# Pairing the value products of windowed attention and moving two batches' masks from TensorE to VectorE

## The chip, the cores and the metric

The kernel is one program on one core of a Trainium2 chip. The metric is device time in microseconds (us), the median of repeated runs of the whole program; a separate profiled execution gives the trace. Five engines work side by side: TensorE (PE in the profile, with its weight loads as PEld), VectorE (DVE), ScalarE (ACT), GpSimd (POOL) and SyncE (SP), which issues the DMAs.

## The reference

Three layers follow one another, all in float32, on 4 batches of 576 tokens.

1. Attention with 8 heads of 64 dimensions. A query sees only keys at or before its own position: in heads 0 to 3 the last 32 positions, in heads 4 to 7 every fourth of the last 128. `scores = where(mask, q k^T / 8, -1e9)`, softmax over the keys, times `v`.
2. A gated channel layer: `x_prev` is `x` shifted by one token; `xk = mu_k x + (1 - mu_k) x_prev`, `xr` alike with `mu_r`; `k = relu(xk w_k)`, `v = k^2 w_v`, result `sigmoid(xr w_r) * v`.
3. A mixer: `u = x + (relu(x^T w_tok1) w_tok2)^T`, result `u + relu(u w_ch1) w_ch2`.

## The kernel before

**Attention in units.** The dilated heads are stored with their tokens sorted by position modulo 4, so that every head has a plain window of 32 keys. Queries are cut into blocks of 64 (`QB`); a block needs 96 keys (`KB`). A unit is four blocks of pairs of heads; `UNITS` lists nine units for each of the four batches, 36 in all, in the order of `RUNS`. `attend(i, ...)` records one unit:

- two DMAs bring queries and keys (`unit`, 416 KB, ring `unit_r`) and values (`vs`, 192 KB, ring `v_r`);
- one bfloat16 matmul of an identity with a slice of `masks` writes 0 or -1e30 into the unit's score bank `sp` (384 columns, line 558), and four float32 matmuls of 96 columns add the scores on top (line 561);
- VectorE takes the negated row maximum (line 565), ScalarE the exponentials with the row sums into `sm` (lines 578 to 582); every second unit of the first batch does this in three wide operations instead; then come the reciprocal and the product `sm * 1/sum` on VectorE;
- four TensorE transposes write `tp`, `copy` brings it to SBUF as `pt`, a ring of two slots (line 592);
- eight matmuls (`vs` by `pt`, 96 rows by 64 columns, lines 595 to 601) write the values' product into `xp`, 256 columns of one bank. Each float32 matmul appears as two records in the trace, so these eight are 16 records. `nc.burst(start)` keeps them in one piece and adds 0.33 to the planner's cost of the first;
- copies bring `xp` to `xT[b, p]`, in the order of tokens (lines 603 to 615).

**The second layer** walks over six chunks of 384 tokens (`CHUNKS`). `prep(c, which, kt)` makes the two shifted mixes of a chunk from `xT` and splits each into a high and a low float32r part; `keys(c, m)`, `mix(c, m, j)` and `receptance(c, j)` multiply with three float32r products for each float32 one (`mm3`). The units of batch 0 come ahead of it; those of the other three are laid beside it by the table `beside` (lines 728 to 731): batch 1 over steps 0 to 9, batch 2 over 10 to 20, batch 3 over 21 to 33, eight steps to a chunk. Chunk 1 needs the first seven units of batch 1, chunk 4 the first seven of batch 3. After step 10 the score bank, the transpose bank and the value bank are one PSUM bank each (lines 725, 741).

**The third layer** follows (lines 769 to 942); its weights are split into high and low parts as their slots come free.

**The order.** Nothing is issued where it is written. Each call is noted as an operation with its dependencies (`Plan.either`), and `Plan.order` simulates the five engines with a table of costs: every TensorE operation has a due time from the written order, every other one the latest time that still serves the operations that need it, and each engine takes the ready operation with the earliest due time. `nc.early` shifts due times (line 549 for the units' DMAs). A burst's first operation takes over the dependencies of the whole group. All instructions are issued from line 392, so groups in the profile are told apart by tile names and shapes: `bank<-x,at 96*64` are the value products from batch 1 on (`x<-wr` and `x<-z` in batch 0), `bank<-cst,at` the transposes, `bank<-at 128x384 bf16` the masks, `bank<-at 128x96` the scores; `bank<-z,wk`, `bank<-wv,z` and `bank<-wr,z` are the second layer.

Of the kernel before, what the change touches and what calls it, by code (L numbers as in the profile page):

```python
# [15 lines left out]
ALU = mybir.AluOpType  # L16
# [6 lines left out]
QB = 64  # L23
# [3 lines left out]
NBLK = 4  # L27
UQ = NBLK * 2 * QB
UK = NBLK * QB + 2 * W
UV = NBLK * 2 * D  # L30
# [11 lines left out]
RUNS = [  # L42
    [(2, 0, 4)], [(2, 4, 4)], [(2, 8, 1), (3, 0, 3)], [(3, 3, 4)], [(3, 7, 2), (0, 0, 2)],
    [(1, 0, 4)], [(0, 2, 4)], [(1, 4, 4)], [(0, 6, 3), (1, 8, 1)],
]
# [7 lines left out]
FIRST = [sum(TILES[:c]) for c in range(len(CHUNKS))]  # L53
CH = 512
NEG = -1.0e30

SLOTS = dict(
    cst=[160], xt=[584] * 12, x2=[2048] * 2 + [1024] * 5, at=[3536, 784, 1216],
# [347 lines left out]
def tile_model(nc, banks, units, cst, mu, w_k, w_v, w_r, w_t1, w_t2, w_c1, w_c2, outT):  # L406
# [14 lines left out]
    def cut(name, numbers, size, count=None):  # L421

        out = []
        for n in numbers:
            out += [(name, n, size * i) for i in range(SLOTS[name][n] // size)]
        return out[:count]

    def ring(*places):
        return Ring(at, sum((p if isinstance(p, list) else [p] for p in places), []))

    def psum(*numbers):
        return Ring(bank, numbers)
# [7 lines left out]
    def copy(out, in_):  # L440
        nc.either(
            ("scalar", "activation", dict(out=out, in_=in_, func=AF.Copy)),
            ("vector", "tensor_copy", dict(out=out, in_=in_)),
        )

    def combine(out, in0, in1, op):
        nc.vector.tensor_tensor(out=out, in0=in0, in1=in1, op=op)
# [86 lines left out]
    masks = table[:, :len(TABLE) * KB // 2].halves().split(len(TABLE), KB)  # L534
    ident_h = table[:, len(TABLE) * KB // 2:].halves()
    unit_r = ring(cut("wv", range(4), UQ + UK), ("z", 4, 0))
    v_r = ring(cut("wr", range(4), UV), ("z", 4, UQ + UK))
# [4 lines left out]
    def attend(i, s_ring, t_ring, x_ring):  # L542

        b, runs = UNITS[i]
        unit, vs = unit_r.tile(UQ + UK), v_r.tile(NBLK, 2, D)[:KB]
        values = units[i][:KB, UQ + UK:].rearrange("p (a b c) -> p a b c", a=NBLK, b=2)
        for out, in_ in ((unit, units[i][:, :UQ + UK]), (vs, values)):
            nc.sync.dma_start(out=out, in_=in_)
            nc.early[len(nc.ops) - 1] = {0: 30, 1: -45}.get(b, 0)
        blocks, o = [], UQ  # L550
        for p, j0, n in runs:
            if j0 == 0:
                nc.gpsimd.memset(out=xT[b, p][:, 0:1], constant=0.0)
            blocks += [(p, j0 + j, unit[:, o + QB * j:o + QB * j + KB]) for j in range(n)]
            o += QB * n + W
        sp, sm, st = s_ring.tile(NBLK, KB), sm_r.tile(NBLK, KB), st_r.tile(4, NBLK)
        row = ROWS[i % len(RUNS)]
        nc.tensor.matmul(out=sp, lhsT=ident_h, rhs=masks[:, row:row + NBLK, :], start=True, stop=False)
        for n, (p, j, ks) in enumerate(blocks):
            qs = unit[:, 2 * QB * n:2 * QB * n + 2 * QB]  # L560
            nc.tensor.matmul(out=sp[:, n, :], lhsT=qs, rhs=ks, start=False, stop=n == NBLK - 1)
            if b:
                nc.early[len(nc.ops) - 1] = -0.5 * n
        scale = 1.0 / np.sqrt(D)
        nc.vector.tensor_reduce(
            out=st[:, 0, :], in_=sp, axis=mybir.AxisListType.X, op=ALU.max, negate=True
        )
        if b == 0 and i % 2:
            nc.vector.tensor_tensor(out=sm, in0=sp, in1=st[:, 0, :].wide(KB), op=ALU.add)
            nc.scalar.activation(out=sm, in_=sm, func=AF.Exp, scale=scale)  # L570
            nc.vector.tensor_reduce(out=st[:, 2, :], in_=sm, axis=mybir.AxisListType.X, op=ALU.add)
        else:
            nc.either(
                ("vector", "tensor_scalar", dict(
                    out=st[:, 1, :], in0=st[:, 0, :], scalar1=scale, scalar2=None, op0=ALU.mult)),
                ("scalar", "activation", dict(out=st[:, 1, :], in_=st[:, 0, :], func=AF.Copy, scale=scale)),
            )
            for j in range(NBLK):
                nc.scalar.activation(
                    out=sm[:, j, :], in_=sp[:, j, :], func=AF.Exp, scale=scale,  # L580
                    bias=st[:, 1, j:j + 1], accum_out=st[:, 2, j:j + 1],
                )
        nc.either(
            ("vector", "tensor_scalar_add", dict(out=st[:, 2, :], in0=st[:, 2, :], scalar1=1e-9)),
            ("scalar", "activation", dict(out=st[:, 2, :], in_=st[:, 2, :], func=AF.Copy, bias=1e-9)),
        )
        nc.vector.reciprocal(out=st[:, 3, :], in_=st[:, 2, :])
        combine(sm, sm, st[:, 3, :].wide(KB), ALU.mult)
        tp, pt = t_ring.tile(NBLK, 2 * QB)[:KB], pt_r.tile(NBLK, 2 * QB)[:KB]
        for j in range(NBLK):  # L590
            nc.tensor.transpose(out=tp[:, j, :], in_=sm[:, j, :], identity=ident)
        copy(pt, tp)
        xp = x_ring.tile(QB * NBLK)
        start = len(nc.ops)
        for j in range(NBLK):
            for hh in range(2):
                r = slice(64 * hh, 64 * hh + 64)
                nc.tensor.matmul(
                    out=xp[r, QB * j:QB * j + QB], lhsT=vs[:, j, hh, :], rhs=pt[:, j, r],
                    start=True, stop=True,  # L600
                )
        nc.burst(start)
        o = 0
        for p, j0, n in runs:
            x, t, end = xT[b, p][:, 1:], QB * j0, QB * (j0 + n)
            if p < 2:
                copy(x[:, t:end], xp[:, o:o + end - t])
                o += end - t
                continue
            x = x.split(S // 4, 4).swap()  # L610
            while t < end:
                c, k = divmod(t, S // 4)
                m = min(end - t, S // 4 - k)
                copy(x[:, c, k:k + m], xp[:, o:o + m])
                t, o = t + m, o + m
# [71 lines left out]
    def mix(c, m, j):  # L687
# [16 lines left out]
        out=om_sb, in0=mu_sb, scalar1=-1.0, scalar2=1.0, op0=ALU.mult, op1=ALU.add  # L704
    )
    diag = []
    for which in range(2):
        diag.append([])
        for kt in range(4):
            diag[which].append([])  # L710
            for k, factor in enumerate((om_sb, mu_sb)):
# [3 lines left out]
                        out=d, in0=ident, scalar1=factor[:, col], scalar2=None, op0=ALU.mult)),  # L715
# [3 lines left out]
    s_ring, t_ring, x_ring = psum(0, 3, 5), psum(1, 6), psum(2, 7)  # L719
    n_units = len(UNITS) // B  # L720
    for i in range(n_units):
        attend(i, s_ring, t_ring, x_ring)


    s_ring, t_ring, x_ring = psum(0, 4), psum(1), psum(2)
    unit_r = ring([("at", 0, (UQ + UK) * i) for i in range(2)])
    v_r = ring([("at", 0, 2 * (UQ + UK) + UV * i) for i in range(3)])
    beside = {}
    for n, (lo, hi) in enumerate(([0, 20], [20, 42], [42, 68])):
        for i in range(n_units):  # L730
# [4 lines left out]
    for g in range(8 * nchunk + 2):  # L735
# [22 lines left out]
        for h in beside.get(2 * g, []):  # L758
            attend(h, s_ring, t_ring, x_ring)
# [5 lines left out]
        for h in beside.get(2 * g + 1, []):  # L765
            attend(h, s_ring, t_ring, x_ring)
# [117 lines left out]
    uhl, mid, op = {}, {}, {}  # L884
# [89 lines left out]
def _constants():  # L974
# [4 lines left out]
    def cut(n):  # L979

        return band & ((i < n) | (j >= W + n))

    first = cut(0)
    blocks = [first, band, cut(16), cut(32), cut(48), cut(-16)]
    masks = np.hstack([np.where(blocks[n], 0.0, NEG) for n in TABLE])
    ident = np.eye(128, dtype=np.float32)
# [34 lines left out]
```

## Time and profile before

| | us |
|---|---|
| median of 3 runs | 734.55 (733.45 to 735.19) |
| the profiled execution | 732.79 |
| its span, first to last instruction | 731.0 |
| PE busy | 715.6 |
| DVE busy | 404.7 |
| ACT busy | 287.1 |

Busy times are unions of an engine's instructions. Matmuls overlap in the profile (one of 384 columns is drawn 0.34 us long while the next starts much earlier), so a matmul's cost is read from the distance between starts, not from its length. The profiled execution lies 1.76 us under the median; 1.79 us of it lie outside the span.

### The profile page before, as it was taken

Reading aid. Unit: us, or ns where it says so; the run is one execution under the profiler, and the core shown is the slowest. Engines: PE = TensorE matmul, PEld = TensorE weight load, DVE = VectorE, ACT = ScalarE, POOL = GpSimd, SP = SyncE. Lnnn points to the kernel's source line nnn. Section 1 sums busy time; section 2 is a strip of 40 time slices with the busy share of each in tenths; the row PEclk is TensorE's granted clock in tenths of the full one; section 3 lists DMA queues with packets and bytes.
Section 4 is the critical chain, followed back from the end, with each engine's and each line's share of the span. In section 5 each row is a group of like instructions: output and inputs, shape, how many; then the busy total and the mean of one; then the engine's idle time right before and its main releaser. Section 6 shows DMA issues by size and latency. Waiting matters only on the chain.

```text
span 731.0 us, 10615 instructions
## 1 busy us (share of the span) xinstructions
PE 715.6 (98%) x4124; PEld 604.6 (83%) x4124; DVE 404.7 (55%) x917; ACT 287.1 (39%) x803; POOL 1.2 (0%) x20
## 2 busy tenths in 40 slices
PE   7699999999999999999999999999999999999998
PEld 6578888888888888988878888888888888888897
DVE  6898898387477388786788898132114112211121
ACT  5776775356244354464466543120112011011110
POOL 0000000000000000000000000000000000000000
PEclk9799999999999999999999999999999999999999
DMA  8946632214122100203321342001000000100010
GB/s 293 323 156 225 196 132 81 67 52 144 47 68 70 46 16 22 73 30 105 98 81 54 96 127 76 1 0 58 1 0 23 35 1 1 57 1 0 1 59 30
DMA packets 26082, 53.84 MB, mean 74 GB/s; under 512 B 2480, under 2 KB 10032, under 8 KB 26032
## 3 DMA queue, kind: packets, MB, share of 16 engines
q1 hardware_dynamic: 26032, 53.17, 22.9%
q8 instruction: 32, 0.52, 0.3%
q14 instruction: 18, 0.15, 0.1%
HBM read 48.44 MB, written 4.72 MB: 73 GB/s over the span
## 4 chain that ended last, share of the span: by engine, by line
PE 95%; DMA 4%; SPq 0%; issue 0%; DVE 0%
PE bank L392 95%; DMA at<-units 2%; DMA wr<-units 1%; DMA wv<-units 1%; SPq L392 0%; DVE z L392 0%
## 5 line engine op out<-in xcount | busy, mean ns | idle before, releaser
L392 PE MATMUL bank<-z,wk 128*128 128x384 f32 (+2 forms) x816 | 196.4, 358 | 0.0
L392 DVE SCALAR_TENSOR_TENSOR z<-bank,z 128x512 fp32r<-128x512 f32 (+2 forms) x116 | 70.4, 607 | 222.3 <-ACT z L392 221.5
L392 ACT ACTIVATE z<-bank 128x512 fp32r<-128x512 f32 (+3 forms) x123 | 65.0, 529 | 285.3 <-PE bank L392 284.3
L392 PEld LDWEIGHTS bank<-z,wk 128*128 128x128 f32 x816 | 146.9, 188 | 15.1 <-ACT x L392 0.3
L392 PE MATMUL bank<-wv,z 128*128 128x512 f32 x432 | 128.9, 405 | 0.0
L392 PE MATMUL bank<-z,x 128*128 128x512 f32 (+1 forms) x540 | 120.2, 371 | 0.0
L392 PEld LDWEIGHTS bank<-z,x 128*128 128x128 f32 x540 | 94.9, 188 | 18.7
L392 PEld LDWEIGHTS bank<-wv,z 128*128 128x128 f32 x432 | 78.3, 189 | 13.8
L392 PE MATMUL bank<-z,at 128*128 128x512 f32 (+2 forms) x300 | 76.9, 388 | 0.0
L392 PE MATMUL bank<-wr,z 128*128 128x512 f32 x216 | 62.8, 406 | 0.0
L392 PEld LDWEIGHTS bank<-z,at 128*128 128x128 f32 (+1 forms) x300 | 52.6, 188 | 11.3 <-issue 1.3
L392 PE MATMUL bank<-at 128*128 128x96 f32 (+1 forms) x252 | 46.3, 284 | 11.0 <-DMA at<-cst 4.9
L392 ACT ACTIVATE at<-bank,at 128x96 f32<-128x96 f32 x128 | 42.4, 340 | 23.7 <-PE bank L392 11.6
L392 DVE TENSOR_TENSOR z<-z,z 128x384 fp32r<-128x384 f32 x88 | 48.1, 554 | 5.8 <-ACT z L392 2.6
L392 PE MATMUL bank<-xt,wk 128*128 128x512 f32 (+2 forms) x176 | 45.2, 387 | 0.0
L392 PEld LDWEIGHTS bank<-wr,z 128*128 128x128 f32 x216 | 39.2, 189 | 6.6
L392 PEld LDWEIGHTS bank<-at 128*128 128x128 f32 x216 | 35.3, 195 | 8.0 <-DMA at<-units 4.1
L392 PE MATMUL bank<-at,z 128*128 128x288 f32 x192 | 35.9, 306 | 0.0
L392 PEld LDWEIGHTS bank<-xt,wk 128*128 128x128 f32 x176 | 30.5, 192 | 6.1
L392 ACT ACTIVATE z<-z 128x384 fp32r<-128x384 f32 x57 | 29.5, 522 | 14.3 <-DVE z L392 8.3
L392 ACT ACTIVATE x<-bank 96x512 f32<-96x512 f32 (+1 forms) x41 | 24.2, 594 | 27.1 <-PE bank L392 26.9
L392 PEld LDWEIGHTS bank<-at,z 128*128 128x128 f32 x192 | 29.7, 188 | 4.0 <-issue 1.8
(106 smaller groups left out, 787.2 us busy)
## 6 DMA issues: line engine op xcount, KB each, us to landing
at<-units SPq DMA_DIRECT2D x27, 416.0 KB, 3.7
wr<-w_c SPq DMA_DIRECT2D x20, 512.0 KB, 3.6
at<-units SPq DMA_DIRECT2D x27, 192.0 KB, 2.6
x<-w_k SPq DMA_DIRECT2D x4, 1024.0 KB, 6.9
x<-w_v SPq DMA_DIRECT2D x4, 1024.0 KB, 7.0
wv<-units SPq DMA_DIRECT2D x8, 416.0 KB, 6.6
outT<-z SPq DMA_DIRECT2D x9, 256.0 KB, 2.0
x<-w_r SPq DMA_DIRECT2D x4, 512.0 KB, 3.6
```

What stands on the lines that cost most here:

```text
L392: call(kw["out"], kw["constant"]) if method == "memset" else call(**kw)
```

## The change

From batch 1 on, `attend` no longer multiplies its own values: it puts the unit on a list, and `weigh` writes the products of two units into the two halves of one bank in one burst (`TOGETHER = 2`; a batch's ninth unit goes alone). In batches 2 and 3 (`MASKED = 2`) the mask matmul is left out; VectorE adds the mask to the scores and writes them to `sm` in SBUF, and the maximum and the exponentials then read `sm`. The ring of the values gets a fourth slot, `y`.

```diff
+MASKED = 2
+TOGETHER = 2
...
-        nc.tensor.matmul(out=sp, lhsT=ident_h, rhs=masks[:, row:row + NBLK, :], start=True, stop=False)
+        mask = masks[:, row:row + NBLK, :]
+        by_pe = b < MASKED
+        if by_pe:
+            nc.tensor.matmul(out=sp, lhsT=ident_h, rhs=mask, start=True, stop=False)
         for n, (p, j, ks) in enumerate(blocks):
             qs = unit[:, 2 * QB * n:2 * QB * n + 2 * QB]
-            nc.tensor.matmul(out=sp[:, n, :], lhsT=qs, rhs=ks, start=False, stop=n == NBLK - 1)
+            nc.tensor.matmul(out=sp[:, n, :], lhsT=qs, rhs=ks, start=not by_pe, stop=n == NBLK - 1 or not by_pe)
...
         scale = 1.0 / np.sqrt(D)
+        if not by_pe:
+            nc.vector.tensor_tensor(out=sm, in0=sp, in1=mask, op=ALU.add)
+            sp = sm
         nc.vector.tensor_reduce(
             out=st[:, 0, :], in_=sp, axis=mybir.AxisListType.X, op=ALU.max, negate=True
         )
...
         copy(pt, tp)
-        xp = x_ring.tile(QB * NBLK)
+        waiting.append((runs, b, vs, pt))
+        if b == 0 or len(waiting) == TOGETHER or (i + 1) % len(RUNS) == 0:
+            weigh(x_ring.tile(2, QB * NBLK))
+
+    waiting = []
+
+    def weigh(xps):
+
         start = len(nc.ops)
-        for j in range(NBLK):
-            for hh in range(2):
-                r = slice(64 * hh, 64 * hh + 64)
-                nc.tensor.matmul(
-                    out=xp[r, QB * j:QB * j + QB], lhsT=vs[:, j, hh, :], rhs=pt[:, j, r],
-                    start=True, stop=True,
-                )
+        for n, (_, _, vs, pt) in enumerate(waiting):
+            for j in range(NBLK):
+                for hh in range(2):
+                    r = slice(64 * hh, 64 * hh + 64)
+                    nc.tensor.matmul(
+                        out=xps[r, n, QB * j:QB * j + QB], lhsT=vs[:, j, hh, :], rhs=pt[:, j, r],
+                        start=True, stop=True,
+                    )
         nc.burst(start)
+        for n, (runs, b, _, _) in enumerate(waiting):
+            place(runs, b, xps[:, n, :])
+        waiting.clear()
+
+    def place(runs, b, xp):
         o = 0
         for p, j0, n in runs:
...
-    v_r = ring([("at", 0, 2 * (UQ + UK) + UV * i) for i in range(3)])
+    v_r = ring([("at", 0, 2 * (UQ + UK) + UV * i) for i in range(3)], ("y", 0, 0))
```

## Rows read from the trace of the kernel before

**Rows 1.** The page: busy time by engine; TensorE's granted clock, 40 slices.
```profile
PE 715.6 (98%) x4124; PEld 604.6 (83%) x4124; DVE 404.7 (55%) x917; ACT 287.1 (39%) x803; POOL 1.2 (0%) x20
...
PEclk9799999999999999999999999999999999999999
```

**Rows 2.** Chain that ended last, in order of time: start, length, what.
```profile
80.16 647.21 PE bank L392 x3601
```

**Rows 3.** Windows: stretch, length, busy by engine (instructions), clock, DMA share, GB/s.
```profile
20.00:40.00 20.00, 13.38 (x117) 9.80 (x115) 17.58 (x32) 14.87 (x44) 0.00 (x0) 0.66 0.93 295
...
160.00:180.00 20.00, 20.00 (x150) 17.09 (x150) 16.98 (x51) 12.41 (x40) 0.00 (x0) 1.00 0.39 115
260.00:280.00 20.00, 20.00 (x145) 16.95 (x144) 17.08 (x45) 12.82 (x36) 0.00 (x0) 1.00 0.05 14
...
120.00:200.00 80.00, 80.00 (x545) 67.88 (x545) 48.24 (x133) 36.45 (x126) 0.00 (x0) 1.00 0.26 74
200.00:280.00 80.00, 80.00 (x543) 69.08 (x542) 55.64 (x136) 38.28 (x126) 0.00 (x0) 1.00 0.16 46
```

**Rows 4.** Timeline of PE round one value burst: start, length, what.
```profile
153.74 0.51 PE L392 MATMUL bank<-z,wk 128*128 128x384 f32 x2
154.18 0.69 PE L392 MATMUL bank<-x,at 96*64 96x64 f32 x16
154.80 0.79 PE L392 MATMUL bank<-z,wk 128*128 128x384 f32 x3
...
155.08 0.51 PE L392 MATMUL bank<-z,wk 128*128 128x384 f32 x2
```

**Rows 5.** Timeline of PE in a plain run of matmuls.
```profile
280.09 2.25 PE L392 MATMUL bank<-z,wk 128*128 128x384 f32 x12
282.18 0.62 PE L392 MATMUL bank<-wv,z 128*128 128x512 f32 x2
```

**Rows 6.** Timeline of PE, two units' bursts in a row (batch 0).
```profile
40.03 0.69 PE L392 MATMUL bank<-x,wr 96*64 96x64 f32 x16
40.54 0.64 PE L392 MATMUL bank<-x,z 96*64 96x64 f32 x16
41.11 1.24 PE L392 MATMUL bank<-xt,wk 128*128 128x384 f32 x3
```

**Rows 7.** Timeline of PE round one mask matmul of batch 2.
```profile
186.62 0.34 PE L392 MATMUL bank<-at 128*128 128x384 bf16 x1
186.65 0.53 PE L392 MATMUL bank<-wv,z 128*128 128x512 f32 x1
187.02 0.24 PE L392 MATMUL bank<-at 128*128 128x96 f32 x1
```

**Rows 8.** Groups by shape: busy us, mean ns, idle before and releasers.
```profile
L392 DVE TENSOR_REDUCE at<-bank 128x4 f32<-128x384 f32 x36 | 19.7, 553 | 19.1 <-PE bank L392 18.7
...
L392 ACT ACTIVATE z<-z 128x384 fp32r<-128x384 f32 x57 | 29.5, 522 | 14.3 <-DVE z L392 8.3 <-PE bank L392 5.5
...
L392 ACT ACTIVATE z<-bank 128x384 f32<-128x384 f32 x48 | 23.5, 491 | 48.2 <-PE bank L392 47.3 <-ACT xt L392 0.7
...
L392 DVE TENSOR_TENSOR at<-bank,at 128x384 f32<-128x384 f32 x4 | 2.2, 550 | 0.0
```

**Rows 9.** Timeline: bursts of batch 1's seventh and eighth unit.
```profile
105.93 0.69 PE L392 MATMUL bank<-x,at 96*64 96x64 f32 x16
...
107.92 0.69 PE L392 MATMUL bank<-x,at 96*64 96x64 f32 x16
```

**Rows 10.** Timeline: batch 3's seventh and eighth unit; the seventh's first use.
```profile
263.87 0.69 PE L392 MATMUL bank<-x,at 96*64 96x64 f32 x16
...
265.26 0.51 ACT L392 ACTIVATE z<-xt,cst 128x256 f32<-128x256 f32 x1
...
272.56 0.69 PE L392 MATMUL bank<-x,at 96*64 96x64 f32 x16
```

**Rows 11.** Timeline of SP: DMA issues, start, length, what.
```profile
34.01 0.42 SPq L392 DMA_DIRECT2D at<-units  x1
...
230.59 23.19 SPq L392 DMA_DIRECT2D at<-units  x5
```

## The prediction

> **What bounds the kernel now.** I read the page first. TensorE is busy 715.6 of 731.0 us, VectorE 404.7 and ScalarE 287.1, and the granted clock is full but for the second of the 40 slices [rows 1]. A drawn length of a matmul overlaps the next, so this share alone proves little; the chain of waits decides. Followed back from the end, it is one piece on TensorE's value and matrix products from 80.16 us on, 647.21 us without a step to another engine [rows 2]. [...] Only the head differs: from 20 to 40 us TensorE is busy 13.38 us at a mean clock of 0.66, and the DMA engines are at 0.93 [rows 3]. So after the head a microsecond taken off TensorE's own stream is a microsecond off the end, and work given to VectorE costs nothing as long as nobody on TensorE waits for it.
>
> **Value bursts.** What a burst costs is read between ordinary matmuls. Twelve of 384 columns advance 2.09 us, 0.174 us each [rows 5]. The two ahead of the burst would be over at 153.74 + 0.35 = 154.09; the burst starts 0.09 later; the next ordinary matmul starts 0.62 after the burst's start, and the one behind it only 0.28 later, 0.106 over its step. The burst thus costs 0.09 + 0.62 + 0.11 = 0.82 us [rows 4]. Two units' bursts in a row already happen once, in batch 0: from the first one's start to the next ordinary matmul 1.08 us [rows 6] against 0.62 [rows 4], so an appended unit costs 0.46. Joining two spares 0.82 - 0.46 = 0.36. The least it can spare are the two gaps outside, 0.09 + 0.11 = 0.20. Batches 1 to 3 have 27 bursts, and will have 4 pairs and one single each: 12 joins. Bounds: 12 x 0.20 = 2.4 and 12 x 0.36 = 4.3 us. I take 0.33, near the upper end, because the joined thing itself was seen [rows 6], and a little under it, because some bursts have narrow neighbours that hide part of a gap: 4.0 us.
>
> The gaps stand where the shape of the array changes, from 128 by 128 to 96 by 64 and back [rows 4]. [...]
>
> **Mask matmuls.** One mask starts at 186.62 and the score after it at 187.02, with one 512-column matmul between [rows 7]. [...] Batches 2 and 3 have 18 units: 18 x 0.17 = 3.1 us (2.9 at least). Its weight load goes with it and is not on the path, for TensorE did not wait around it.
>
> **What VectorE gets.** One add of 384 columns from PSUM a unit. The nearest row, the same shape from PSUM with a second operand in SBUF, takes 0.55 us [rows 8]; that the mask is bfloat16 I cost at nothing, bounded above by nothing better than that row. 18 x 0.55 = 9.9 us more. The maximum keeps its 0.55 us [rows 8]. The cover is VectorE's idle time: 80 - 48.24 and 80 - 55.64 in the two halves, and 3.0 and 2.9 us in their two fullest 20 us [rows 3], where at most three units' adds, 1.7 us, fall. If the cover were gone, a unit's chain would be 0.55 us longer, and that would count only where TensorE has nothing else ready.
>
> **What ScalarE gets.** 72 exponentials read SBUF in place of PSUM. The 384-column copies on ScalarE take 522 ns from SBUF and 491 from PSUM [rows 8], so about 0.03 us each, 2.2 us in all; below that nothing. ScalarE idles over half of both halves [rows 3]. In exchange the score bank, one bank for all units here, comes free after the add and not after the last exponential, so the next unit's scores may start earlier.
>
> **Waits that move.** The products of a pair's first unit wait for the second: its copies to `xT` come one unit later. This matters where a chunk needs unit seven of a batch (chunks 1 and 4), because units seven and eight form a pair. In batch 1 the two bursts stand at 105.93 and 107.92, 2.0 us apart [rows 9]; in batch 3 at 263.87 and 272.56, 8.7 us apart, and the mix of chunk 4 reads the seventh's output at 265.26 [rows 10]. The planner sees this: the burst's first operation takes over all dependencies of the pair, so the eighth unit's whole chain gets the due time of the seventh's output. Its scores can be moved up, since the five DMAs of units between 230.59 and 253.78 are the last before that point [rows 11], and TensorE's choice of other ready work is wide. I take no stall; bounds are 0 and 2.0 + 8.7 = 10.7 us.
>
> The two `pt` slots are both held until the burst, so the next pair's first `pt` copy waits for it, and with it whatever is queued behind it on its engine; units are several us apart, and the burst follows the second copy at once. The value bank now holds two units, and the next pair's burst waits for the copies of both, some 16 us after them at the pace of batch 3 [rows 10]. Neither is costed.
>
> SyncE's queue keeps its length. With four slots a value load waits for a burst no later than before. The new slot is free from the start, so one load can be issued near the others at 34.01 [rows 11] rather than behind a burst; it is 192 KB, 0.67 us at the 295 GB/s of that stretch [rows 3], and a weight load queued behind it may land that much later: 0 to 0.7 us, I take nothing.
>
> **Sum.** 4.0 + 3.1 = 7.1 us off the profiled execution's 732.79 gives 725.7. That execution lies 1.76 us under the median of the runs, so against the median 734.55 - 7.1 = 727.5 us. By the lower bounds 2.4 + 2.9 = 5.3 and 729.3, by the upper 4.3 + 3.1 = 7.4 and 727.1. About 0.2%, 1.5 us, is what a measurement of this kernel can tell from no change.
>
> **The rivals.**
> *Only the outer gaps are spared* (a joined unit pays its own slow start): 2.4 + 3.1 = 5.5, 729.1 us. Against it stand the 1.08 us of the joined pair [rows 6]; for it, that this is a single case, in the head. [...] Chance 0.12.
> *The pair's wait reaches TensorE.* The eighth unit isn't moved up enough and chunk 4's, less likely chunk 1's, key products come late. For it: in batch 3 the mix follows its input within 2 us, and the two bursts are 8.7 us apart [rows 10]. Against it: due times carry the need back, and TensorE found other work through all of this stretch [rows 3]. Partly, with 1.5 to 4.5 us of stall, about 730.5 us: 0.14. Wholly, 10.7 - 7.1 = 3.6 us slower than before, 738.2 us: 0.06. It decides from 7.1 us of stall on, and is told from no change above 8.6.
> *VectorE becomes the bound* in batches 2 and 3: all 9.9 us of adds end up in front of TensorE, 2.8 us slower, 737.4 us. It would need its idle 31.8 and 24.4 us [rows 3] to be unusable; 0.04.
> *The head is reordered.* All due times move by some tenths, and the first 40 us have 6.6 us of idle TensorE and a lowered clock in one 20 us window [rows 3], which a late load can lengthen or an early one shorten: 2 us either way, 725.5 or 729.5; 0.06.
>
> **How the numbers follow.** The forecast keeps 0.58, with a range of its own of 726.3 to 729.0 (bounds of the two savings and the run-to-run spread). The time given is its own. The range goes to 725.3 on the lucky side of the head and to 731.8 over most of the partial stall; left out are the full stall, VectorE as the bound and the tails, under 2 in 10. Faster by over 0.2%: forecast, outer gaps, nearly all of the partial stall, the head, 0.87. Within 0.2%: stalls of 5.6 to 8.6 us, 0.05. Slower: full stall and VectorE less their milder cases, 0.08.
>
> **What the changed profile would show.** In batches 1 to 3 12 value bursts of 32 records and 3 of 16, about 1.08 us from a pair's start to the next ordinary matmul; 18 bfloat16 matmuls, not 36; `TENSOR_TENSOR at<-bank,at` of 384 columns 22 times, near 0.55 us, and VectorE's busy time up by some 10 us; TensorE without idle time after the head. The prediction is wrong if TensorE waits for `z` of chunk 1 or 4 (the wait of the pair), if the joined burst takes over 1.2 us, if the first 45 us last longer or shorter by over 1 us, or if other stretches of TensorE get gaps that were not there.

## The result, and the profile after

The changed kernel takes 726.88 us (median of 4 runs, 725.28 to 728.77) against 734.87 us for the kernel before beside it (733.45 to 735.40). The ratio is 0.9895, interval 0.9867 to 0.9924: of 734.87 us that is 7.7 us less, 5.6 to 9.8. The profiled execution took 725.28 us with a span of 723.5, against 732.79 and 731.0: 7.5 us less in one pair of executions. The forecast was 7.1 us and 727.5. One of the twelve executions of experiment 1, the profiled one, ran in a slow state (1170.07 us at a mean granted clock of 0.558) and is counted nowhere below.

First the page of the kernel after: busy time by engine, and the clock granted to TensorE in 40 slices, as in [rows 1].

```profile
PE 707.9 (98%) x4106; PEld 603.7 (83%) x4106; DVE 407.3 (56%) x918; ACT 294.9 (41%) x820; POOL 1.1 (0%) x20
...
PEclk9799999999999999999999999999999999999999
```

TensorE has 18 instructions and 7.7 us of drawn time less; the clock is as it was. VectorE has only 2.6 us more, not the 10 that were forecast, and ScalarE 7.8 us more. The groups below show where that comes from.

The chain that ended last, its two long pieces in order of time (start, length, what):

```profile
29.87 4.29 PE bank L394 x40
34.18 685.67 PE bank L394 x3895
```

The piece of [rows 2] that begins at 80.16 us has one more of TensorE ahead of it in the kernel before, with 0.01 us between the two:

```profile
29.70 50.45 PE bank L392 x352
```

So in both kernels the chain stays on TensorE from some 30 us on, with no step to another engine: nothing of what the change added ended up in front of TensorE after the head. The windows say the same (stretch, length, busy time and instructions of PE, PEld, DVE, ACT and POOL, clock, DMA share, GB/s):

```profile
100.00:120.00 20.00, 20.00 (x152) 17.77 (x151) 18.01 (x45) 14.95 (x52) 0.00 (x0) 1.00 0.31 95
120.00:200.00 80.00, 80.00 (x557) 70.64 (x556) 52.99 (x142) 40.79 (x143) 0.00 (x0) 1.00 0.28 84
200.00:280.00 80.00, 80.00 (x551) 70.62 (x550) 59.05 (x144) 43.28 (x138) 0.00 (x0) 1.00 0.14 44
```

Against [rows 3], TensorE is as full as before and starts 12 and 8 matmuls more in the two long stretches (120 to 200 and 200 to 280 us, the two halves of the prediction, where batches 2 and 3 run), VectorE has 4.8 and 3.4 us more, ScalarE 4.3 and 5.0. The row from 100 to 120 us is read again with the sixth experiment: there VectorE is already at 18.01 of 20 us.

A joined burst, from the timeline of PE (start, length, what):

```profile
223.24 1.15 PE L394 MATMUL bank<-x,at 96*64 96x64 f32 x32
224.32 1.43 PE L394 MATMUL bank<-wv,z 128*128 128x512 f32 x5
```

From 223.24 to 224.32 are 1.08 us for two units, the number that batch 0 had shown [rows 6]. There are 12 such bursts of 32 records and 3 of 16 behind batch 0, as forecast; in six of the twelve one half reads the slot `y` and is drawn as a row of its own.

**Where the time went.** Single executions differ by a few us in the head, where the first loads land: in the thirteen traces that are used here the last burst of batch 0 starts between 39.57 and 42.69 us. So I measure from a point behind it: from the last value burst of batch 0, `bank<-x,z`, to the last row of two 512-column `wv` matmuls ahead of the first 512-column `bank<-z,at`. All attention lies in between. In the kernel before the stretch begins at 40.54 [rows 6] and ends with this row:

```profile
361.58 0.71 PE L392 MATMUL bank<-wv,z 128*128 128x512 f32 x2
```

In the kernel after:

```profile
39.99 0.64 PE L394 MATMUL bank<-x,z 96*64 96x64 f32 x16
...
354.26 0.71 PE L394 MATMUL bank<-wv,z 128*128 128x512 f32 x2
```

The stretch is 321.04 us before and 314.27 after, 6.77 less. The head ends 0.55 us earlier, and what follows the stretch differs by 0.18 (731.0 - 361.58 = 369.42; 723.5 - 354.26 = 369.24); 6.77 + 0.55 + 0.18 = 7.5, the whole difference of the spans. One correction belongs to it: the kernel before had done eight records of batch 1's 96-column score matmuls ahead of the stretch's start, the kernel after four. Such a record takes some 0.09 us from start to start (the mean of 206 in the kernel before), so the stretch before is 0.36 us short of work, and on equal work the saving in it is 6.77 + 0.36 = 7.1 us. Apart from these four score records and the 18 masks the two stretches hold the same matmuls.

**What VectorE and ScalarE exchanged.** Groups by shape of the kernel after (x count, busy us and mean ns, idle before and releasers):

```profile
L394 ACT ACTIVATE z<-z 128x384 fp32r<-128x384 f32 x60 | 30.5, 520 | 12.4 <-PE bank L394 6.2 <-DVE z L394 5.8
L394 ACT ACTIVATE at<-at 128x96 f32<-128x96 f32 x72 | 26.1, 364 | 3.6 <-DVE at L394 3.3
L394 ACT ACTIVATE at<-bank,at 128x96 f32<-128x96 f32 x56 | 18.4, 338 | 3.9 <-DVE at L394 3.0 <-PE bank L394 0.6
L394 ACT ACTIVATE x<-bank 96x512 f32<-96x512 f32 x28 | 16.6, 595 | 10.8 <-PE bank L394 10.6
...
L394 DVE TENSOR_TENSOR at<-bank,at 128x384 f32<-128x384 f32 x22 | 12.2, 556 | 13.8 <-PE bank L394 13.7
L394 DVE TENSOR_REDUCE at<-at 128x4 f32<-128x384 f32 x22 | 12.0, 547 | 0.2
...
L394 DVE TENSOR_REDUCE at<-bank 128x4 f32<-128x384 f32 x18 | 9.9, 552 | 7.1 <-PE bank L394 6.7
...
L394 PE MATMUL bank<-at 128*128 128x384 bf16 x18 | 6.2, 380 | 9.0 <-DMA at<-cst 5.0 <-ACT at L394 4.0
...
L394 DVE COPY x<-bank 96x512 f32<-96x512 f32 x8 | 5.5, 685 | 5.8 <-PE bank L394 5.8
```

And of the kernel before, two groups that stand beside the `pt` copies, `x<-bank`:

```profile
L392 ACT ACTIVATE x<-bank 96x512 f32<-96x512 f32 x24 | 14.2, 594 | 11.8 <-PE bank L392 11.5
...
L392 DVE COPY x<-bank 96x512 f32<-96x512 f32 x12 | 8.2, 685 | 17.4 <-PE bank L392 17.4
```

The adds are there: 22 against 4 [rows 8], 18 x 0.556 = 10.0 us. But of the 36 `pt` copies VectorE now makes 8 in place of 12, and ScalarE makes 28 in place of 24; three more of the 384-column casts are ScalarE's too (57 [rows 8] to 60), and eight more of the first mix products. These are the operations that the code offers to either engine; the planner's order moved them. The exponentials from SBUF take 364 ns, 26 more than the 338 from PSUM; 72 x 0.026 = 1.9 us, and some 1.1 of that comes back in the reads behind them (last section). So nearly all of ScalarE's 7.8 us is moved work.

### The profile page after: what moved, and what is told of

The parts are those of the page before. It is cut to its first block, busy times and chain, and to the rows that moved or that the text cites. A ratio compares the mean times of both kernels' runs of the same rounds, so it can differ in the third digit from the quotient of the medians.

```text
span 723.5 us, 10575 instructions
## 1 busy us (share of the span) xinstructions
PE 707.9 (98%) x4106; PEld 603.7 (83%) x4106; DVE 407.3 (56%) x918; ACT 294.9 (41%) x820; POOL 1.1 (0%) x20
## 4 chain that ended last, share of the span: by engine, by line
PE 95%; DMA 4%; SPq 0%; issue 0%; DVE 0%
PE bank L394 95%; DMA at<-units 2%; DMA wr<-units 1%; DMA wv<-units 1%; SPq L394 0%; DVE z L394 0%
## 5 line engine op out<-in xcount | busy, mean ns | idle before, releaser
L394 PE MATMUL bank<-z,wk 128*128 128x384 f32 (+2 forms) x816 | 200.0, 358 | 0.0
L394 PEld LDWEIGHTS bank<-z,at 128*128 128x128 f32 (+1 forms) x300 | 52.6, 188 | 11.3 <-issue 1.3
L394 PE MATMUL bank<-at 128*128 128x96 f32 (+1 forms) x234 | 40.9, 276 | 11.5 <-DMA at<-cst 5.0
L394 ACT ACTIVATE x<-bank 96x512 f32<-96x512 f32 (+1 forms) x45 | 26.8, 596 | 34.1 <-PE bank L394 33.7
L394 ACT ACTIVATE at<-at 128x96 f32<-128x96 f32 (+2 forms) x107 | 34.4, 324 | 8.2 <-DVE at L394 7.5
```

The source lines that it names most:

```text
L394: call(kw["out"], kw["constant"]) if method == "memset" else call(**kw)
```

## The experiments

Two theories stood at the start. The one of the prediction: TensorE's own stream is the bound, the joined bursts give some 4 us and the masks some 3, and VectorE's adds are hidden. Against it: one of the two parts gives nothing or all, because the outer gaps alone are spared, or because the adds or the pair's wait give back what TensorE saved. Letters in the expectations name theories as each expectation introduces them. Ratios are against the kernel before on the same chip; the stretch is the one measured above, 314.27 us in the kernel after.

**1. The pairs alone.**

```
-MASKED = 2
+MASKED = 4
```

> All masks stay on TensorE; the value products are still written two units at a time, with the fourth slot. Theory A (what counts is what leaves TensorE's stream): 12 joins at 0.33 to 0.36 us, 4.0 to 4.3 us under the kernel before, and in the profile 12 value bursts of 32 records, about 1.08 us each from start to the next ordinary matmul. Theory B (only the outer gaps are spared): 2.4 us under it. Theory C (the gain of the whole change is the luck of a new order, mostly in the first 45 us): no fixed share; the stretch after 46 us would be as long as before and the head shorter.

Measured: 730.54 us, the median of eleven executions, ratio 0.9954 (0.9938 to 0.9970): 3.4 us faster (2.2 to 4.6). The pairs do give a part, and not the whole. The rows of this kernel are those of experiment 8, taken later.

**2. The masks alone.**

```
-TOGETHER = 2
+TOGETHER = 1
```

> Each unit multiplies its own values, VectorE adds the masks of batches 2 and 3, four value slots. Theory A: 18 mask matmuls at 0.17 us, 3.1 us under the kernel before, TensorE without idle time after the head. Theory D (VectorE's 9.9 us of adds come partly to lie in front of TensorE): less than 2 us under it, or over it, with idle time on TensorE between 115 and 280 us. Theory C: no fixed share.

Measured: 730.38 us, ratio 0.9960 (0.9947 to 0.9973): 2.9 us faster (2.0 to 3.9). Its stretch runs between these rows of PE's timeline:

```profile
40.94 0.63 PE L394 MATMUL bank<-x,z 96*64 96x64 f32 x16
...
359.32 0.71 PE L394 MATMUL bank<-wv,z 128*128 128x512 f32 x2
```

It is 318.38 us. Its stretch holds the same number of matmuls of every shape as that of the kernel after, so the difference 318.38 - 314.27 = 4.11 us is what joining twelve bursts gives when everything else stays: 0.34 us a join. Against the kernel before it is 2.66 us shorter, with the 0.36 of the four score records 3.0.

**3. The add made twice.** Each of the 18 units gets a second add of the mask, in place, between the first add and the maximum. The scores so carry the mask twice.

```
             nc.vector.tensor_tensor(out=sm, in0=sp, in1=mask, op=ALU.add)
+            nc.vector.tensor_tensor(out=sm, in0=sm, in1=mask, op=ALU.add)
```

> The changed kernel, but VectorE adds the mask a second time, in place in SBUF, so the work that was moved to VectorE is doubled (18 more operations of about 0.55 us, 9.9 us; the masked scores are more negative, the softmax is the same). Theory A: the time of the changed kernel, 727 us, within 1 us, since VectorE idles enough. Theory D: several us over the changed kernel, up to 9.9.

Measured: 727.45 us, ratio 0.9916 (0.9902 to 0.9931), an interval that overlaps that of the change. Rows of PE's timeline:

```profile
42.69 0.63 PE L394 MATMUL bank<-x,z 96*64 96x64 f32 x16
...
356.86 0.71 PE L394 MATMUL bank<-wv,z 128*128 128x512 f32 x2
```

The stretch is 314.17 us, 0.10 less than without the second add. Doubling the whole suspected cost, 18 x 0.55 = 9.9 us more in the units' chains, cost TensorE nothing; the execution's longer span is all in its head, which ends 2.7 us later. So the adds are free here, and VectorE is no bound in batches 2 and 3.

**4. The mask on both engines.** TensorE adds the mask in all batches as before, and VectorE adds it again in batches 2 and 3. The scores there carry it twice.

```
-        if by_pe:
-            nc.tensor.matmul(out=sp, lhsT=ident_h, rhs=mask, start=True, stop=False)
+        nc.tensor.matmul(out=sp, lhsT=ident_h, rhs=mask, start=True, stop=False)
...
-            nc.tensor.matmul(out=sp[:, n, :], lhsT=qs, rhs=ks, start=not by_pe, stop=n == NBLK - 1 or not by_pe)
+            nc.tensor.matmul(out=sp[:, n, :], lhsT=qs, rhs=ks, start=False, stop=n == NBLK - 1)
```

> The changed kernel, but TensorE multiplies the mask in batches 2 and 3 too, as before; VectorE adds it once more. Theory A: 3.1 us over the changed kernel, about 730 us, and TensorE's busy time 3 us up. If the mask matmuls had been hidden beside other matmuls they would cost nothing and the time would be 727 us.

Measured: 728.88 us, ratio 0.9934 (0.9916 to 0.9951). Rows of PE's timeline:

```profile
41.38 0.63 PE L394 MATMUL bank<-x,z 96*64 96x64 f32 x16
...
358.62 0.71 PE L394 MATMUL bank<-wv,z 128*128 128x512 f32 x2
```

317.24 - 314.27 = 2.97 us come back with the 18 matmuls, 0.165 us each, on the same other work in the stretch. The adds are in both kernels, so this is the mask matmul's price alone. It is 0.165 us though a mask is drawn 0.34 [rows 7] to 0.38 us long: a matmul's length in the profile is not its share of the stream.

**5. The single unit first.** With nine units a batch has four pairs and one single. Here the single is the first one, so that units seven and eight no longer form a pair.

```
-        if b == 0 or len(waiting) == TOGETHER or (i + 1) % len(RUNS) == 0:
+        if b == 0 or len(waiting) == TOGETHER or i % len(RUNS) == 0:
```

> The changed kernel, but a batch's first unit goes alone and its last eight in pairs, so that unit seven, on which chunks 1 and 4 wait, is the second of its pair and waits for nobody. As many bursts and masks as in the changed kernel. Theory A (the planner moved unit eight up, the pair's wait costs nothing): the changed kernel's time, 727 us, within 1 us, and from the last value burst of batch 0 to the last product with w_v the same 314.2 us within 0.5. Theory E (the pair's wait takes back part of the gain): 1 us or more less in that stretch.

Measured: 725.94 us, ratio 0.9905 (0.9885 to 0.9924), stretch 314.14 us against 314.27. The pair of seven and eight, on which the mixes of chunks 1 and 4 wait, costs nothing that can be seen.

**6. The masks of the second batch as well.**

```
-MASKED = 2
+MASKED = 1
```

> The changed kernel, but VectorE adds the masks of batch 1 too (MASKED = 1), in the stretch from 46 to 120 us, where it is busy some 66 of 74 us. Theory A: 9 more mask matmuls leave TensorE, 9 x 0.17 = 1.5 us under the changed kernel, if VectorE's 5.0 us of adds find room. Theory D (VectorE is nearly the bound there): nothing gained or up to 3.4 us lost, with waits of TensorE between 60 and 120 us.

Measured: 726.48 us, ratio 0.9902 (0.9884 to 0.9920), stretch 314.36 us. Nine more mask matmuls are gone, seven of them out of the stretch (the kernel after had done the other two ahead of it): 7 x 0.165 = 1.2 us, and nothing was gained. Two rows of PE's timeline (in brackets the idle time before and what ended it), and a window:

```profile
105.51 0.98 PE L394 MATMUL bank<-wv,z 128*128 128x512 f32 x3 [0.26 <-ACT wv L394]
...
107.44 1.88 PE L394 MATMUL bank<-wv,z 128*128 128x512 f32 x7 [0.22 <-DVE wv L394]
```

```profile
100.00:120.00 20.00, 19.51 (x144) 16.57 (x142) 19.45 (x50) 16.44 (x51) 0.00 (x0) 1.00 0.26 73
```

VectorE is busy 19.45 of 20 us, and TensorE waits for operands that VectorE and ScalarE round. Here, where this window of the kernel after showed 18.01, there is hardly any cover left. The waits that the window draws are 20.00 - 19.51 = 0.49 us. A drawn wait understates what it costs, since a matmul is drawn longer than it advances the stream (one of 384 columns 0.34 us against 0.174 [rows 5]): counted from start to start, the two places are 0.42 and 0.44 us longer than the same neighbours are elsewhere in these traces. That is 0.86 of the 1.2 us. The remaining 0.4 is open.

**7. Three slots for the values.**

```
-    v_r = ring([("at", 0, 2 * (UQ + UK) + UV * i) for i in range(3)], ("y", 0, 0))
+    v_r = ring([("at", 0, 2 * (UQ + UK) + UV * i) for i in range(3)])
```

> The changed kernel with the three value slots of before. A pair then holds two of three slots until its burst, and the values of the pair's second successor are loaded only after it. Theory A: a load takes under 4 us and units come some 8 us apart, so the fourth slot is worth nothing that can be measured: 727 us within 1 us. Theory F (the fourth slot is needed for pairing): TensorE waits for value loads before bursts, 1 us or more over the changed kernel.

Measured: 725.27 us, ratio 0.9888 (0.9872 to 0.9904), stretch 314.27 us, to the hundredth that of the change. The fourth slot is worth nothing here.

**8. The kernel of experiment 1 once more, one execution with its rows.** Same edit.

> The kernel with pairs alone (masks on TensorE in all batches), for a profile at full clock. Theory A: from the last value burst of batch 0 to the last product with w_v 320.9 - 12 x 0.33 = 317.0 us, and 12 bursts of 32 records. Theory B (only the outer gaps are spared): 320.9 - 2.4 = 318.5.

Measured: 730.73 us, span 729.0, stretch 318.80 us: 2.24 less than before, where experiment 2 gives 4.1 for twelve joins. Its bursts are as in the kernel after, 12 of 32 matmuls in 1.08 us. The waits of PE between 40 and 75 us (what waited for what: us in total, times, longest) say where the rest went:

```profile
PE bank L394 <- ACT xt L394: 1.6, 1, 1.6
PE bank L394 <- DVE z L394: 0.5, 1, 0.5
```

2.1 us of idle TensorE, ahead of the first pair at 64.79, which neither the kernel before nor the one after has there. 2.24 + 2.1 = 4.3; its head had done eight score records and one mask more than that of the kernel before, 8 x 0.09 + 0.17 = 0.89, which flatters the stretch. That leaves some 3.4 us for the joins, 0.29 each, from one execution and with the waits at their drawn length. So the joins give most of what experiment 2 shows for them (0.34), and this kernel lost a part of it again at the start of batch 1, in waits that stand ahead of its first joined burst. Why the planner's order came out so with the masks on TensorE wasn't followed.

**9. Pairs in the first batch too.**

```
-        if b == 0 or len(waiting) == TOGETHER or (i + 1) % len(RUNS) == 0:
+        if len(waiting) == TOGETHER or (i + 1) % len(RUNS) == 0:
```

> The changed kernel, but batch 0's units are paired as well, 4 more joins, in the head, where TensorE is not the bound. Theory A (a join is worth its gaps only where TensorE is full): no gain, and the head, up to the last value burst of batch 0 at 40.4 us, lasts 0 to 3 us longer since copies to xT come a unit later. If TensorE's work counted there too: 1.4 us under the changed kernel.

Measured: 725.21 us, ratio 0.9879 (0.9858 to 0.9900). The median is the lowest of all, but the interval overlaps that of the change widely. In its one trace the last burst of batch 0 starts at 41.81 against 39.99, behind one wait of 5.1 us for the units' load, against 2.5 in the kernel after. In the traces of the kernel before and of experiments 2, 3, 4, 7 and 10 that wait is 2.8 to 3.8 us, so single executions differ in it, and neither a gain nor a loss is shown.

**10 to 12. The pair's wait, made longer.** The eighth unit's scores are planned later by a dose of 9, 18 or 25 us, in batches 1 to 3, so that the first of the pair waits longer for the second.

```
-                nc.early[len(nc.ops) - 1] = -0.5 * n
+                nc.early[len(nc.ops) - 1] = -0.5 * n - 9 * (i % len(RUNS) == 7)
```

> The changed kernel, but the scores of each batch's eighth unit (batches 1 to 3) are due 9 us later in the planner's eyes, about where batch 3's eighth unit stood before, so that the pair's second half comes late for chunks 1 and 4. It tells why the pair's wait cost nothing. Theory A (the planner moved unit eight up): the wait comes back, 1 to 5 us over the changed kernel, with TensorE waiting for the mixes of chunk 4 near 265 us or of chunk 1 near 105 us. Theory G (it would have cost nothing anyway, since TensorE has other ready work): 727 us within 1 us.

Measured: 727.59 us, ratio 0.9907 (0.9884 to 0.9929). The dose did not reach the burst: batch 3's pair starts at 264.71, as far behind the head as in the kernel after (263.40). This run tells nothing of the wait; its stretch is 314.21 us, as in the change. With 18 in place of 9:

> As e10, with 18 in place of 9, since with 9 the eighth unit did not move: batch 3's seventh and eighth unit are now to be multiplied some 8 us later than in the changed kernel. Theory A (the planner's moving unit eight up is what kept the pair's wait off TensorE): 2 to 8 us over the changed kernel, with gaps of TensorE near 110 or 270 us. Theory G (TensorE has other ready work for so long): 727 us within 1.5 us.

Measured: 726.97 us, ratio 0.9901 (0.9882 to 0.9921). Two rows of PE's timeline:

```profile
271.47 1.15 PE L394 MATMUL bank<-x,at 96*64 96x64 f32 x32
...
275.16 0.80 PE L394 MATMUL bank<-z,wk 128*128 128x384 f32 x3 [0.24 <-DVE z L394]
```

The pair comes at 271.47, measured from the head some 7.4 us later than in the kernel after, and TensorE idles 0.24 us behind it; batch 1's pair comes 6.8 us later, with one wait of 0.30 behind it. The stretch is 315.03 us, 0.76 longer. Seven us of delay of the seventh unit's output are almost wholly covered by other ready matmuls. With 25:

> As e11 with 25, a second dose: the pair comes some 13 us later than in the changed kernel. Theory A and theory G both let the wait reach TensorE here, by 5 us or more over the changed kernel (G: only what exceeds TensorE's stock of other work). If nothing is lost even now, the seventh unit is not needed when the mixes of chunk 4 say so.

Measured: 733.03 us, ratio 0.9995 (0.9982 to 1.0008): all of the gain is lost. Rows of PE's timeline:

```profile
109.18 1.10 PE L394 MATMUL bank<-at 128*128 128x96 f32 x8 [1.38 <-DMA at<-units]
...
115.85 0.69 PE L394 MATMUL bank<-at 128*128 128x96 f32 x4 [0.52 <-DVE at L394]
...
119.04 0.64 PE L394 MATMUL bank<-cst,at 128*96 128x128 f32 x4 [0.99 <-DVE at L394]
...
132.53 1.15 PE L394 MATMUL bank<-x,at 96*64 96x64 f32 x32
...
194.22 0.69 PE L394 MATMUL bank<-x,y 96*64 96x64 f32 x16
...
274.32 1.44 PE L394 MATMUL bank<-x,at 96*64 96x64 f32 x32
...
277.62 0.69 PE L394 MATMUL bank<-x,at 96*64 96x64 f32 x16 [1.29 <-ACT at L394]
278.52 0.44 PE L394 MATMUL bank<-z,wk 128*128 128x384 f32 x1 [0.22 <-ACT z L394]
279.17 3.44 PE L394 MATMUL bank<-z,wk 128*128 128x384 f32 x12 [0.20 <-DVE z L394]
282.76 0.95 PE L394 MATMUL bank<-z,wk 128*128 128x384 f32 x2 [0.16 <-DVE z L394]
```

Windows of the same trace, and two rows of PE's timeline in the kernel after:

```profile
275.00:278.00 3.00, 1.65 (x35) 1.35 (x35) 2.56 (x7) 1.90 (x7) 0.00 (x0) 1.00 0.02 4
280.00:282.00 2.00, 2.00 (x8) 2.00 (x7) 2.00 (x7) 2.00 (x6) 0.00 (x0) 0.53 0.02 4
```

```profile
129.43 1.15 PE L394 MATMUL bank<-x,at 96*64 96x64 f32 x32
...
178.45 0.69 PE L394 MATMUL bank<-x,y 96*64 96x64 f32 x16
```

The stretch is 321.84 us, 7.6 longer, but the dose stands in three batches, and the loss comes in two places. The first pair of batch 2 is already 3.5 us late behind the head (132.53 against 129.43): so much was lost beside batch 1, whose pair of seven and eight comes 9.9 us later. Batch 2's own pair comes 16.2 us later (194.22 against 178.45) and adds nothing, for the first pair of batch 3 is again 3.5 us late. The other 4.1 us come beside batch 3, whose pair at 274.32 is some 11.3 us later than in the kernel after.

Drawn as waits are 4.8 us. The four large ones, 1.38 + 0.52 + 0.99 + 1.29 = 4.2, are for a load of a unit, a softmax with no cover and a `pt` copy; the key products of chunk 4 (`bank<-z,wk`) wait only 0.22 + 0.20 + 0.16 us for `z`. In these windows TensorE was busy 1.65 of 3.00 us from 275 to 278 at a granted clock of 1.00, and from 280 to 282 the clock was 0.53. The twelve key products from 279.17 on advance 3.43 us up to the wait behind them, where the twelve of [rows 5] advance 2.09: 1.3 us more, of which 2.00 x (1 - 0.53) = 0.9 are an estimate for the lower clock of that window. The remaining 1.4 us weren't found. So a late pair can reach TensorE, as the prediction's largest rival had it: hardly with 7 us of added delay, but with 10 and 11. This experiment makes the whole eighth unit late, not only the pair's wait for it, and what the wait for chunk 4 alone would cost isn't separated.

None of the versions beats the change by more than its interval. Undoing the wait of the pair (5) or the slot (7), or adding pairs (9) or masks (6), gives medians between 725.2 and 726.5 with overlapping intervals.

## Why the prediction was right, step by step

**What bounds the kernel** held: the saving of TensorE's stream came out of the span one for one, 7.1 us on equal work in the stretch for 7.1 costed, and the two parts measured apart add up to it, 4.11 (experiment 2) + 2.97 (experiment 4) = 7.1. The 0.55 us of the head in the traced pair come on top of that and are luck of one execution.

**Value bursts.** 12 joins at 0.33 were costed at 4.0 us; measured 4.11, 0.34 a join (experiment 2 against the change). The rival that only the outer gaps are spared would have given 2.4 and falls. What the joined burst already showed once in batch 0 [rows 6] was the better measure than the gaps seen around a burst [rows 4]. Of what a join spares, 0.20 us are these outer gaps; the other 0.15 lie inside. Record by record, the second pair of records of the burst in [rows 4] starts 0.107 us behind the first and the others follow 0.058 apart, so the start has 0.05; from the last pair to the next ordinary matmul it is 0.159, so the end has 0.10. No run shows that narrow neighbours hide part of a gap, for which the prediction went a little under 0.36: in the trace before, two score matmuls advance 0.13 us ahead of an ordinary one (82.48 to 82.61) and 0.29 ahead of a burst (82.99 to 83.28), 0.16 more, where the ordinary neighbour of [rows 4] has 0.09.

**Masks.** 18 at 0.17 were costed at 3.1: 0.40 us from a mask's start to the score behind it [rows 7], less 0.174 x 512 / 384 = 0.23 [rows 5] for the matmul between. Measured 2.97, 0.165 each (experiment 4). No run shows the 2.9 us that the prediction takes as the least for the masks; 2.97 is what came, and a float32 matmul of as many columns advances 0.174 [rows 5].

**VectorE.** The price of an add, 0.55 us, was right (0.556), and so was that it is hidden (experiment 3). Wrong was the statement of what would be seen: "VectorE's busy time up by some 10 us". It rose by 2.6, because operations that either engine can do moved to ScalarE, which got 7.8 us instead of the 2.2 costed. The step that failed is that the rest of the work was taken to stay where it is. It had no effect on the time, since ScalarE had room as well. How much room there is also bears on experiment 6: one batch earlier VectorE is at 18.01 of 20 us, ScalarE at 14.95, and taking masks off TensorE gains nothing; two waits for their operands account for some 0.9 of the 1.2 us.

**ScalarE's exponentials.** 0.03 us each were costed, 0.026 measured, 364 ns from SBUF against 338 from PSUM. On VectorE the reduction of 384 columns took 547 ns from SBUF and 552 from PSUM, 5 ns less.

**The pair's wait.** Zero was taken, and experiment 5 shows no more than the 0.13 us by which its stretch differs. Of the two reasons given, one is shown: TensorE does find other work, for some 7 us more than it needed (11), though not for 10 and 11 (12). The `pt` slots and the value bank, which the prediction left uncosted, cost nothing either: between 40 and 354 us TensorE has no drawn wait in the kernel after. The bound of 8.7 us from batch 3 was too large, and for a reason that the trace before shows. The eighth unit's softmax was over long ahead of its burst at 272.56 [rows 10]; its last product stands here in VectorE's timeline:

```profile
257.63 0.55 DVE L392 TENSOR_TENSOR at<-at 128x384 f32<-128x384 f32 x1
```

The transposes stood 13 us behind it and the burst 15, though every operand was there. A distance between two bursts in a planned order is a choice, not a readiness; the wait that a pair can force is at most the distance to the last operand. In the kernel after that product is at 249.32, the pair at 263.40 and the mix of chunk 4 at 265.07, as early as before [rows 10]:

```profile
249.32 0.55 DVE L394 TENSOR_TENSOR at<-at 128x384 f32<-128x384 f32 x1
...
265.07 0.51 ACT L394 ACTIVATE z<-xt,cst 128x256 f32<-128x256 f32 x1
```

That due times pulled the eighth unit forward fits these rows; it was not tested by itself.

**Slots, queue and head.** The fourth slot and the queue of loads were costed at nothing, and taking the slot away changed nothing (7). The head came 0.55 us earlier in the traced pair, within the 2 us allowed.

## What to carry to other kernels

Where one engine is full without a gap, cost a change by that engine's stream alone, from the distance between starts of neighbouring rows, never from drawn lengths; here a joined burst was forecast at 0.33 us and gave 0.34, a dropped mask at 0.17 and gave 0.165. Then ask how much room the engines beside it have in the narrowest stretch, not on average: the same trade gave 0.165 us an instruction in batches 2 and 3 and nothing in batch 1, where VectorE was at 18 of 20 us. And in an order made by a planner, a long distance between two steps may be slack that was never needed: read when the operands were ready before pricing a wait by it.

## What the hardware showed unexpectedly

The read of the accumulator that follows each exponential is also a little different by source: 189 ns when the exponential read SBUF against 204 when it read PSUM, so that 15 of the 26 ns come back:

```profile
L394 ACT ACTIVATION_READ_ACCUMULATOR at<-at 128x1 f32 x72 | 13.6, 189 | 0.0
L394 ACT ACTIVATION_READ_ACCUMULATOR at<-bank,at 128x1 f32 x56 | 11.4, 204 | 0.0
```

An exponential of 96 columns with its sum thus costs 553 ns from SBUF and 542 from PSUM, 11 ns more and not 26.

The granted clock fell far from any change, in one execution and not in another. The trace of experiment 10 has 1.5 us more than the others behind the stretch (726.3 - 355.54 = 370.8 us against 369.2 to 369.5). There, in the third layer, the clock granted to TensorE is 0.50 from 413 to 416 us, with TensorE busy 3.00 of these 3.00 us; in the kernel after it is 1.00 from 412 to 416. A window of experiment 10 and one of the kernel after:

```profile
413.00:416.00 3.00, 3.00 (x13) 3.00 (x14) 1.79 (x4) 0.95 (x3) 0.00 (x0) 0.50 0.00 0
```

```profile
412.00:416.00 4.00, 4.00 (x28) 3.79 (x27) 3.55 (x8) 1.37 (x5) 0.00 (x0) 1.00 0.06 11
```

What lets it fall there isn't shown. A difference of a us or two between single executions is therefore no effect of a change until the rows show where it lies.
